# An adaLN transformer block on one core: five steps of a hand-written schedule moved by a slot or a few

## The chip, the core and the metric

The kernel runs on one core of a Trainium2 chip. A core has a matrix engine (PE, with its weight loads shown apart as PEld), a vector engine (DVE), a scalar engine (ACT), a general engine (POOL) and a sync engine (SP), which here issues nearly all DMAs. The metric is the device time of one execution in microseconds (us). Each kernel is run several times; the median of the runs is compared.

## The reference

One block with adaptive LayerNorm: attention over the last 512 cached keys, then a gated feed-forward layer. S is 2048 rows, D is 512, there are 32 query heads and 8 key/value heads of 128, and F is 1792. All is float32.

```python
mod = (silu(c) @ w_mod).reshape(1, 6, 1, 512)
sa, ca, ga, sb, cb, gb = (mod[:, i] for i in range(6))
h = layernorm(x) * (1 + ca) + sa
q = heads(h @ wq)                                   # 32 heads of 128
k, v = k_cache[:, :, -512:, :], v_cache[:, :, -512:, :]   # each serves 4 heads
p = softmax(q @ k.T * 128 ** -0.5)
x = x + ga * (merge(p @ v) @ wo)
h = layernorm(x) * (1 + cb) + sb
x = x + gb * ((gelu(h @ w_gate) * (h @ w_up)) @ w_down)
```

## The kernel before

**Numbers.** Every float32 operand of a large product is split into a high and a low float16 part; `mm3` (line 87, where all the products stand as L91) makes one product of three float16 matmuls. A split is two instructions: the high part is a copy on ACT, the low part a subtraction on DVE or POOL.

**Strassen-like combinations.** The query projection and the feed-forward layer use seven block products for eight. They need the normalised activations in blocks `b11, b21, y, b22` (plain) and `t1, t2, t3, t4` (combined). The activations are written to DRAM as float32 (`hs`), and `combos` (line 570) later loads them back as tiles `cb` (`load`), subtracts them from one another on POOL (`diff`, L582, `cb<-cb`), and splits the results into the blocks (high part on ACT at L380, low part on POOL at L384). `combos(gen, p, ...)` yields four pairs of a load and its steps. `gen` counts uses: 0 and 1 are the first and second 1024 rows for attention, 2 and 3 the first and second 1024 rows for the feed-forward layer; `p` is 0 or 1.

**Attention.** There are 128 units (a head pair's head, a row block of 512) of four slots; slot `t` runs from 0 to 511 (`T` is 512). In a slot PE makes the scores `ps` of 128 rows, DVE takes their maximum (`nm`, L990), ACT the exponential (`ee`, L999) and, two slots later, the high part of the probabilities (`p`, L1011), DVE, three slots later, their low part (L1016), and SP a DMA transpose of both (`pt<-p`, L1020). The DMA transposes are counted T0 to T511 here, one for each slot; T(t-3) is issued in slot t. The product with V (`po`) of a unit needs all four of its transposes and comes two units later. Beside it PE makes the next queries (`qa, qb, qc, pq`) and the output projection (`py`), three groups of matmuls in each slot from a queue.

**Order.** Nothing is left to a scheduler here: `at(("w", t), fn)` puts a step at the end of slot t, on whatever engines its instructions use, and each engine runs its instructions in that order. Loads into pools with few buffers go through `sched(pos, (load, steps), ..., ahead=AHEAD)`: the steps run at the slots given, and the load is issued `ahead` slots (3) before the first one, or when the buffer is released by the numbers of the schedule, if that is later. Pools are served in order of the first step's slot, so a load can wait behind another one. `spare` issues one waiting background DMA (stores of split weights, `kept<-...`, and fetches of them) in a slot that has moved nothing else.

**LayerNorm of the second half.** When the attention output of a row tile `ti` is complete (`attn_final`, slots 256 to 290 for the tiles 0 to 7), `ln_tile(2, ti, ...)` gives seven steps: `stat`, `norm` (POOL), `turn` (four PE transposes into a PSUM bank `pln`, L508), `affine` of columns 0 and 1 and of columns 2 and 3 (two ACT instructions each, `hf<-pln`, L516, the second one also stores to `hs`), and two splits. They are placed at offsets from the slot in which the tile is complete:

```python
for d, fn in zip((1, 5, 8, 9, 10, 12, 13), steps):
    at(("w", now[0] + d), fn)
```

The bank `pln` comes from the pool `acc` of five PSUM banks, which are taken in turn.

**Feed-forward weights.** `prep_set(q, b)` (line 1372) splits one pair of weight blocks (q even: gate, q odd: up) in the slots from `b` on, on ACT, PE, DVE and POOL, into four `stage` tiles, and stores these to DRAM for much later. Its two loads go into the pool `rw`, which has two buffers (`NRW`); the split is `made(k)` on POOL (L159, L160), the last reads of the two buffers are `made(1)` and `made(2)`.

```python
for n in range(NP):
    b = T // 2 + 30 + 27 * n
    prep_set(2 * n, b)
    prep_set(2 * n + 1, b + 13)
    prep_wd(n, b + 21)
```

**Feed-forward.** After slot 512 there are 28 items of seven products each (`fa, fb, fc`), and between them the down projection in two halves of seven products (`ya, yb, yc`). `step(q, fn)` puts a step behind product `q % 7` of item `q // 7`. DVE adds each finished `y` product into `yt` (L1687). The bank `ya` takes part in four products of a half, and PE may go on in it only after DVE has read it. `combos(3, 1, ...)`, the last combinations, are loaded at step 70, for products from step 98 on. DVE forms `gelu(gate) * up` at L1294 (`fg`), POOL the combinations of that at L1320.

Of the kernel before, what the change touches and what calls it, by code (L numbers as in the profile page):

```python
# [26 lines left out]
QT = QB // P  # L27
EPS = 1e-5
SCALE = DH ** -0.5
AHEAD = 3  # L30
# [35 lines left out]
def block_kernel(ctx: ExitStack, tc: tile.TileContext, x, kT, v, wq, wo, wg, wu, wd, cT, wc, wm, out):  # L66
    nc = tc.nc
# [10 lines left out]
    def raw(name):  # L78
        return pool.tile([P, 512], F32, tag="raw", name=name, bufs=NRAW)
# [15 lines left out]
    def dma(out_, in_):  # L95
        moved[0] += 1
        nc.sync.dma_start(out_, in_)
# [276 lines left out]
    def stored(gen, name, p):  # L374
        qb, dt = {"b11": (0, p), "b21": (0, 2 + p), "y": (1, p), "b22": (1, 2 + p)}.get(name, (None, None))
        return spilled(gen, name)[:, p, :] if qb is None else spilled(gen, qb)[:, dt, :]
# [193 lines left out]
    def combos(gen, p, eng, base=True, d=0, e=0):  # L570
        X = {}

        def load(name):
            if gen == 0 and (p == 0 or name in ("b21", "b22")):
                X[name] = kept({"b11": "s1", "y": "u2", "b21": "u3"}[name]) if name != "b22" else \
                    pool.tile([P, 512], F32, tag="w2", name="cb", bufs=2)
            else:
                X[name] = raw("cb")
            dma(X[name], stored(gen, name, p))

        def diff(o, a, b):
            return lambda: nc.gpsimd.tensor_tensor(X[o], X[a], X[b], op=ALU.subtract)  # L582

        def parts(pos, name, tile_):
            high, low = put(gen, name, p, lambda: X[tile_], eng)
            return [(pos, high), (pos + 1 + e, low)]

        def plain(pos, name):
            return parts(pos, name, name) if base else []

        return [
            (lambda: load("b11"), plain(0, "b11") + [(2, diff("b11", "y", "b11"))] + parts(d + 4, "t1", "b11")),
            (lambda: load("y"), [(2, nop), (3, diff("y", "b22", "y"))] + parts(d + 5, "t3", "y")),
            (lambda: load("b22"), (plain(1, "b22") or [(2, nop)]) + [(4, diff("b22", "b22", "b11"))] + parts(d + 6, "t2", "b22")),
            (lambda: load("b21"), plain(3, "b21") + [(5, diff("b21", "b21", "b22"))] + parts(d + 7, "t4", "b21")),
        ]
# [19 lines left out]
    def sched(pos, ld, *more, kind="raw", ahead=AHEAD):  # L616
        loads.append(((pos,) + more, ld, kind, ahead))
# [121 lines left out]
    def at(key, *fns):  # L739
        later.setdefault(key, []).extend(fns)  # L740
# [154 lines left out]
    def kept(k):  # L895
        return pool.tile([P, QB], F32, tag=k, name=k, bufs=1)
# [69 lines left out]
    def attn_final(ti):  # L966
        y1[ti] = dram.tile([P, D], F32, name=f"y{ti}")
        dma(y1[ti], acc[ti])
        if ti < 2 * QT:
            nxt = ti + 2 * QT  # L970
            own, steps = ln_tile(2, ti, lambda: acc[ti])
            own()
            for d, fn in zip((1, 5, 8, 9, 10, 12, 13), steps):
                at(("w", now[0] + d), fn)
            at(now[0] + 12, lambda: load_acc(nxt, rows_of(x, nxt)))
        else:
            ln_last(ti - 2 * QT)
# [204 lines left out]
    def sched_combos(gen, p, base):  # L1182
        for k, (load, steps) in enumerate(combos(gen, p, nc.gpsimd if gen or p == 0 else nc.vector, False, 0 if gen else 1 if p else 2, 0 if gen or p else 5)):
            if gen == 0 and (p == 0 or k > 1):
                at(base + ((0, 0, 0, 2)[k] if p else (-10, -2, -1, -9)[k]), load)
                for off, fn in steps:
                    at(("w", base + off), fn)
            else:
                sched(base + steps[0][0], (load, [fn for _, fn in steps]), *[base + off for off, _ in steps[1:]])

    for p in range(2):
        sched_combos(0, p, CB[p])
# [25 lines left out]
    for g in range(NG):  # L1218
# [6 lines left out]
        if 0 < g < GW:  # L1225
            a, b = plain_steps(g, by)
            sched_pair(g, srcs, t0 - (19 if g > 1 else 13), spread, [(t0 - (13 if g > 1 else 8), a)], [(t0 - (11 if g > 1 else 7), b)])
        elif g >= GW and (not half or pr < GW):
            sched_set(g, srcs, t0, by, spread)
            if not half:  # L1230
                a, b, c, d, e, f = SETPOS2 if g == GW else SETPOS
# [11 lines left out]
        else:  # L1243
            if g > 0:
                if pr % 2 == 0:
                    load, stat, spread_, parts = k_items(pr)
                    sched(t0 - (22 if g > 2 else 20), (load, [stat]))
                    at(("w", t0 - (19 if g > 2 else 17)), spread_)
                load, stat, spread_, parts = k_items(pr)
                sched(t0 - (7 if g > 2 else 8 if g > 1 else 6), (load, [parts if g != 2 else lambda parts=parts: soon(parts(True))]))  # L1250
                at(t0 - (3 if g > 2 else 1 if g > 1 else 2), lambda pr=pr: store(("k", pr), KV[0, pr, 0]))
                if pr % 2 == 0:
                    load, stat, spread_, parts = v_items(qd)
# [118 lines left out]
    def prep_set(q, b):  # L1372
        m, key, by = {}, ("f", q), col("fsc", f_scale(q))
        l, r = slice(0, 256), slice(256, 512)
        outs = [staged() for _ in range(4)]
        srcs = set_srcs(q)

        def tt(o, a, c, op):
            nc.gpsimd.tensor_tensor(o, a, c, op=op)

        def made(k, src):
            halves(outs[k][0]["t"] if k < 3 else outs[k][0]["t"][:, :, 0:256], src)

        def keep_it(k):
            return lambda: store(("w", key, k), outs[k][0]["t"] if k < 3 else outs[k][0]["t"][:, :, 0:256], 0)

        def s0():
            times(RAW[key][0], by)
            made(0, RAW[key][0])

        def s1():
            r1 = RAW[key][1]
            times(r1, by)
            made(3, r1[:, r])
            tt(r1[:, r], r1[:, l], r1[:, r], ALU.add)

        def s2():
            r0, r1 = RAW[key][0], RAW[key][1]
            tt(r1[:, l], r0[:, l], r1[:, l], ALU.subtract)
            tt(r0[:, l], r1[:, r], r0[:, l], ALU.subtract)  # L1400
            tt(r0[:, r], r0[:, r], r0[:, l], ALU.subtract)

        sched(b, (lambda: set_load(key, srcs, 0), [lambda: pair_stat(key, m, 0), nop]), b + 9, kind="rw")
        sched(b + 1, (lambda: set_load(key, srcs, 1), [lambda: pair_stat(key, m, 1), lambda: f_spread(f_scale(q), m["m"]), s2, nop]),
              b + 4, b + 9, b + 10, kind="rw")
        sched(b + 7, (outs[0][1], [s0, keep_it(0)]), b + 10)
        sched(b + 8, (outs[3][1], [s1, keep_it(3)]), b + 11)
        sched(b + 9, (outs[1][1], [lambda: made(1, RAW[key][0]), keep_it(1)]), b + 12)
        sched(b + 10, (outs[2][1], [lambda: made(2, RAW[key][1]), keep_it(2)]), b + 13)
# [65 lines left out]
    for n in range(NP):  # L1475
        b = T // 2 + 30 + 27 * n
        prep_set(2 * n, b)
        prep_set(2 * n + 1, b + 13)
        prep_wd(n, b + 21)
    for n, b in ((NP - 2, T - 57), (NP - 1, T - 22)):  # L1480
        prep_wd(n, b, True)
# [165 lines left out]
    def step(q, fn):  # L1647
        f_at(q // 7, q % 7, fn)

    for i, q in enumerate((16, 19, 22, 26, 30, 33, 36, 40)):  # L1650
        load, norm, split, turn = ln_turned(i)
# [3 lines left out]
        step(q + 4, turn)  # L1655
    for q, (qb, dt) in zip((37, 41, 44, 47, 50, 51, 54, 55), ((0, 0), (0, 2), (0, 1), (0, 3), (1, 0), (1, 2), (1, 1), (1, 3))):
        step(q, lambda qb=qb, dt=dt: turned_out(qb, dt))
    for p, (q, at_) in enumerate(((59, (61, 62, 62, 63, 64, 65, 66, 67, 68)), (70, (75, 76, 76, 79, 80, 81, 82, 89, 90)))):
        for load, steps in combos(3, p, nc.gpsimd):
            step(q, load)  # L1660
            for off, fn in steps:
                step(at_[off], fn)

    def whole(ti):
        if ti in halfway and ti in joined:
# [117 lines left out]
    for q in range(NQ):  # L1783
        n, m = divmod(q, 2)
# [55 lines left out]
```

## Time and profile before

| | |
|---|---|
| median of 3 runs | 1733.44 us (1733.02 to 1733.84) |
| the profiled execution | 1734.19 us, of which 1732.4 us from its first to its last instruction |
| PE busy | 1711.2 us, 99% |
| DVE, ACT, POOL busy | 82%, 72%, 63% |
| granted TensorE clock | 0.999 |
| DMA | 343.51 MB, mean 198 GB/s |

In the timeline a row is: start, duration, engine, line, operation, output<-input and their kind, the number of instructions merged, and in brackets the idle time before it with what ended it. PE's matmuls overlap: their ends are modelled, and a row of three matmuls of 512 columns reads 0.81 us while the next row begins 0.65 us after it. SPq rows are issues of DMAs; a transfer's landing is another number.

### The profile page before, as it was taken

The numbers are of one execution on the slowest core, as the hardware profiler recorded it, in microseconds if no ns is written. First come the engines' busy times: TensorE is split into PE (matmuls) and PEld (weight loads), VectorE is DVE, ScalarE is ACT, GpSimd is POOL, SyncE is SP. The second block draws the span as 40 slices with busy tenths as digits, with TensorE's granted clock in tenths as the row PEclk, the third lists the DMA queues.
The fourth block names the chain that finished last, engine by engine and source line by source line (L and its number), as shares of the span: only waits on it lengthen the run. The fifth ranks groups of instructions, "written<-read, shape, count | busy, mean of one in ns | idle before, by whom it ended". The sixth has DMA issues, their size and how long they took to land.

```text
span 1732.4 us, 26343 instructions
## 1 busy us (share of the span) xinstructions
PE 1711.2 (99%) x8012; PEld 787.1 (45%) x8012; DVE 1425.8 (82%) x2476; ACT 1254.3 (72%) x2819; POOL 1093.3 (63%) x1328
## 2 busy tenths in 40 slices
PE   7999999999999999999999999999999999999998
PEld 5444444444444444444444444444444444444444
DVE  7888898988888899888888888888896788676666
ACT  6988788888888777897787777787785354455442
POOL 4879778777788884655665755747760345735424
PEclk9999999999999999999999999999999999999999
DMA  7999999999999998999999999999997556355353
GB/s 234 218 208 210 214 214 205 225 205 220 211 229 222 206 210 181 219 207 224 198 232 219 206 231 208 203 218 221 229 227 164 163 145 196 118 164 174 96 157 104
DMA packets 693454, 343.51 MB, mean 198 GB/s; under 512 B 579136, under 2 KB 602688, under 8 KB 693312
## 3 DMA queue, kind: packets, MB, share of 16 engines
q1 hardware_dynamic: 693024, 341.30, 85.4%
q8 instruction: 63, 1.03, 0.3%
q14 instruction: 79, 0.65, 0.1%
q10 hardware_dynamic: 288, 0.52, 0.1%
HBM read 137.50 MB, written 63.70 MB: 116 GB/s over the span
## 4 chain that ended last, share of the span: by engine, by line
PE 86%; DVE 5%; ACT 4%; POOL 2%; DMA 2%; issue 1%; SPq 0%; POOLq 0%; DVEq 0%; ACTq 0%
PE py L91 18%; PE po L91 17%; PE ps L91 16%; PE fa L91 8%; PE qa L91 8%; PE fc L91 4%; PE qc L91 4%; PE ya L91 3%; PE fb L91 2%; PE qb L91 2%; PE yc L91 2%; ACT ee L999 1%; DVE p L1016 1%; DVE nm L990 1%; ACT p L1011 1%
## 5 line engine op out<-in xcount | busy, mean ns | idle before, releaser
L999 ACT ACTIVATE ee<-ps,nm 128x512 f32<-128x512 f32 x512 | 349.6, 683 | 184.2 <-DVE nm L990 181.0
L1016 DVE SCALAR_TENSOR_TENSOR p<-ee,rr,p 128x512 f16<-128x512 f32 x512 | 454.1, 887 | 8.1 <-ACT p L1011 7.5
L990 DVE TENSOR_REDUCE nm<-ps 128x1 f32<-128x512 f32 x512 | 350.3, 684 | 105.7 <-PE ps L91 102.9
L91 PE MATMUL ps<-k,qt 128*128 128x512 f16 x1536 | 414.9, 379 | 3.8 <-ACT ee L999 2.5
L1011 ACT ACTIVATE p<-ee,rr 128x512 f16<-128x512 f32 x512 | 363.9, 711 | 21.9 <-DMA pt<-p 11.6
L91 PE MATMUL po<-pt,v 128*128 128x512 f16 x1536 | 372.9, 379 | 2.8 <-DVE kmax L184 1.0
L91 PE MATMUL py<-wo,ot 128*128 128x512 f16 x1536 | 371.3, 379 | 0.0
L91 PEld LDWEIGHTS <-w 128*128 128x128 f16 x2184 | 214.0, 98 | 259.7 <-issue 2.7
L91 PEld LDWEIGHTS <-v 128*128 128x128 f16 x1536 | 149.9, 98 | 185.1 <-issue 5.1
L91 PEld LDWEIGHTS <-ot 128*128 128x128 f16 x1536 | 150.3, 98 | 181.2
L91 PEld LDWEIGHTS <-qt 128*128 128x128 f16 x1536 | 145.8, 98 | 174.8 <-issue 3.3
L1320 POOL TENSOR_TENSOR fg<-fg 128x512 f32<-128x512 f32 x48 | 63.0, 1312 | 147.0 <-DVE fg L1294 144.2
L748 DVE SCALAR_TENSOR_TENSOR ot<-po,ot 128x512 f16<-128x512 f32 x128 | 87.8, 686 | 37.7 <-ACT ot L747 37.3
L1304 ACT ACTIVATE at<-fg 128x512 f16<-128x512 f32 x92 | 56.3, 626 | 80.1 <-DVE fg L1294 61.7
L999 ACT ACTIVATION_READ_ACCUMULATOR ee<-ps,nm 128x1 f32 x512 | 100.1, 195 | 0.0
L960 DVE SCALAR_TENSOR_TENSOR acc<-py,ysc,acc 128x512 f32<-128x512 f32 x128 | 94.7, 740 | 5.3 <-PE py L91 5.3
L91 PE MATMUL qa<-t,w 128*128 128x512 f16 x348 | 84.9, 379 | 0.0
L236 POOL TENSOR_TENSOR lw<-lw,half__86 128x1 f32<-128x1 f32 x39 | 25.0, 641 | 91.0 <-DVE lw L186 91.0
L91 PE MATMUL fa<-t,w 128*128 128x512 f16 x336 | 81.7, 379 | 0.1
L747 ACT ACTIVATE ot<-po 128x512 f16<-128x512 f32 x128 | 73.9, 577 | 5.0 <-PE po L91 5.0
L403 POOL TENSOR_TENSOR rs<-rs,nhalf 128x1 f32<-128x1 f32 x32 | 18.7, 586 | 92.9 <-DVE rs L397 90.0
L91 PEld LDWEIGHTS <-wo 128*128 128x128 f16 x504 | 49.3, 98 | 60.6 <-issue 1.3
(243 smaller groups left out, 2821.9 us busy)
## 6 DMA issues: line engine op xcount, KB each, us to landing
w<-kept SPq DMA_DIRECT2D x123, 256.0 KB, 3.3
wo<-kept SPq DMA_DIRECT2D x72, 256.0 KB, 3.3
kept<-stage SPq DMA_DIRECT2D x67, 256.0 KB, 3.2
raw<-in_wo SPq DMA_DIRECT2D x56, 256.0 KB, 3.2
kept<-w SPq DMA_DIRECT2D x39, 256.0 KB, 3.3
rw<-in_wq SPq DMA_DIRECT2D x38, 256.0 KB, 3.1
hs<-hf SPq DMA_DIRECT2D x32, 256.0 KB, 2.8
pt<-p SPq DMA_TRANSPOSE x512, 3.5
```

Of the source, the lines that this page charges most:

```text
L91: nc.tensor.matmul(ps, a, b, start=first and n == 0, stop=last and n == 2, skip_group_check=chain)
L236: nc.gpsimd.tensor_tensor(out, out, half_, op=ALU.pow)
L403: nc.gpsimd.tensor_tensor(st["rs"], st["rs"], nhalf, op=ALU.pow)
L747: nc.scalar.activation(t[:, 0, :], src, AF.Copy, scale=scale)
L748: return lambda: nc.vector.scalar_tensor_tensor(t[:, 1, :], src, scale, t[:, 0, :], op0=ALU.mult, op1=ALU.subtract)
L960: nc.vector.scalar_tensor_tensor(acc[ti], st["p"], by, acc[ti], op0=ALU.mult, op1=ALU.add)
L990: nc.vector.tensor_reduce(nm, E[t]["ps"], axis=AX.X, op=ALU.max, negate=True)
L999: nc.scalar.activation(e, E[t]["ps"], AF.Exp, bias=E[t]["nm"], scale=1.0, accum_out=sm[:, t % 2:t % 2 + 1])
L1011: nc.scalar.activation(p16[:, 0, :], E[t]["e"], AF.Copy, scale=E[t]["r"])
L1016: nc.vector.scalar_tensor_tensor(p16[:, 1, :], E[t]["e"], E[t]["r"], p16[:, 0, :], op0=ALU.mult, op1=ALU.subtract)
L1304: nc.scalar.activation(t[:, 0, :], g, AF.Copy)
L1320: nc.gpsimd.tensor_tensor(g[o], g[a], g[b], op=ALU.subtract)
```

## The change

Four places of the schedule are edited; no computation is added or taken away, and each engine executes the same instructions as before.

1. In `sched_combos`, the four loads of the combinations of the generations 1 and 2 get their own distances before the first step, 3, 2, 1 and 3 slots, where each had 3.
2. In `attn_final`, for `ti` 2 and 6, the second pair of affine pieces is put in the same slot as the first (offset 9 for 10).
3. The second `prep_set` of n = 0 begins one slot later (`b + 14`); all its steps move by one slot.
4. The steps of `combos(3, 1)` get a table for each of the four tiles. The subtraction into `y` moves from step 79 to 81, that into `b22` from 80 to 82, that into `b21` from 81 to 89; the split of `t3` (`y`) from 81/82 to 83/89, of `t2` (`b22`) from 82/89 to 88/89 and of `t4` (`b21`) from 89/90 to 95/96 (high part / low part).

```diff
             own, steps = ln_tile(2, ti, lambda: acc[ti])
             own()
-            for d, fn in zip((1, 5, 8, 9, 10, 12, 13), steps):
+            for d, fn in zip((1, 5, 8, 9, 9, 12, 13) if ti % QT == QT - 2 else (1, 5, 8, 9, 10, 12, 13), steps):
                 at(("w", now[0] + d), fn)
...
     def sched_combos(gen, p, base):
...
             else:
-                sched(base + steps[0][0], (load, [fn for _, fn in steps]), *[base + off for off, _ in steps[1:]])
+                sched(base + steps[0][0], (load, [fn for _, fn in steps]), *[base + off for off, _ in steps[1:]], ahead=(3, 2, 1, 3)[k] if gen else AHEAD)
...
         prep_set(2 * n, b)
-        prep_set(2 * n + 1, b + 13)
+        prep_set(2 * n + 1, b + (13 if n else 14))
...
-    for p, (q, at_) in enumerate(((59, (61, 62, 62, 63, 64, 65, 66, 67, 68)), (70, (75, 76, 76, 79, 80, 81, 82, 89, 90)))):
-        for load, steps in combos(3, p, nc.gpsimd):
-            step(q, load)
-            for off, fn in steps:
-                step(at_[off], fn)
+    for load, steps in combos(3, 0, nc.gpsimd):
+        step(59, load)
+        for off, fn in steps:
+            step((61, 62, 62, 63, 64, 65, 66, 67, 68)[off], fn)
+    for (load, steps), at_ in zip(combos(3, 1, nc.gpsimd), ((75, 76, 76, 80, 81), (76, 81, 83, 89), (76, 76, 82, 88, 89), (79, 80, 89, 95, 96))):
+        step(70, load)
+        for (_, fn), k in zip(steps, at_):
+            step(k, fn)
```

**Place one: SP around the transposes T197 to T201** (edit 1, generation 1, p = 0). `cb<-hs` are the loads of the combinations, `rw<-in_wq` those of the next query weights, `kept<-wo` a background store. Before:

```order
L1020 DMA_TRANSPOSE pt<-p_7010 128x8x128
L97 DMA cb<-hs_1_5325 128x512
L97 DMA cb<-hs_0_3160 128x512
L97 DMA cb<-hs_1_5325 128x512
L1020 DMA_TRANSPOSE pt<-p_7039 128x8x128
L97 DMA rw<-in_wq 128x512
L97 DMA kept<-wo 128x1024
L1020 DMA_TRANSPOSE pt<-p_7073 128x8x128
L97 DMA rw<-in_wq 128x512
L1020 DMA_TRANSPOSE pt<-p_7108 128x8x128
```

The same place after the change:

```order
L1020 DMA_TRANSPOSE pt<-p_7010 128x8x128
L97 DMA kept<-wo 128x1024
L1020 DMA_TRANSPOSE pt<-p_7039 128x8x128
L97 DMA cb<-hs_1_5325 128x512
L97 DMA cb<-hs_0_3160 128x512
L97 DMA rw<-in_wq 128x512
L1020 DMA_TRANSPOSE pt<-p_7068 128x8x128
L97 DMA cb<-hs_1_5325 128x512
L97 DMA rw<-in_wq 128x512
L1020 DMA_TRANSPOSE pt<-p_7106 128x8x128
```

The four transposes are T197 to T200. The three loads in one gap have become none, two and one in three gaps (the pool's order keeps the first two together), and the store has moved up. Between T197 and T199 stand five other DMAs and T198 before, four and T198 after. In generation 2 the loads around T475 and T485 move by one slot in the same way; with them a weight fetch moves from before T476 to before T479 and a fetch of V from before T479 to before T481. In generation 1, p = 1, nothing moves.

**Place two: ACT and SP around T290 to T296** (edits 2 and 3). First ACT, one piece of the difference, for `ti` 6; the piece for `ti` 2, some 16 slots earlier, reads alike. `hf<-pln` are the affine pieces, `qt` the high part of the next queries:

```order
 L1011 ACTIVATE p_10040<-ee,rr 128x512
-L516 ACTIVATE hf<-pln,cols 128x128 x2
-L999 ACTIVATE ee,sm<-ps,nm 128x512
-L1004 ACTIVATE rr<-sm 128x2
-L1011 ACTIVATE p_10074<-ee,rr 128x512
-L747 ACTIVATE qt<-qd,qsc 128x512
-L516 ACTIVATE hf<-pln,cols 128x128 x2
+L516 ACTIVATE hf<-pln,cols 128x128 x4
+L999 ACTIVATE ee,sm<-ps,nm 128x512
+L1004 ACTIVATE rr<-sm 128x2
+L1011 ACTIVATE p_10075<-ee,rr 128x512
+L747 ACTIVATE qt<-qd,qsc 128x512
```

The third and fourth affine piece now stand ahead of the next exponential. Their store `hs<-hf` moves one transpose earlier on SP. Then SP from T293 to T296 (edit 3); `rw<-in_wu` are the two loads that come a slot later, `kept<-stage` stores of the set prepared before. Before:

```order
L1020 DMA_TRANSPOSE pt<-p_10146 128x8x128
L97 DMA rw<-in_wu 128x512
L97 DMA kept<-stage 128x1024
L97 DMA hs_1_9778<-hf 512x1x128
L1020 DMA_TRANSPOSE pt<-p_10183 128x8x128
L97 DMA rw<-in_wu 128x512
L97 DMA kept<-stage 256x1x256
L1020 DMA_TRANSPOSE pt<-p_10218 128x8x128
L97 DMA acc<-in_x 128x512
L97 DMA kept<-stage 128x1024
```

After:

```order
L1020 DMA_TRANSPOSE pt<-p_10146 128x8x128
L97 DMA kept<-stage 128x1024
L97 DMA hs_1_9778<-hf 512x1x128
L1020 DMA_TRANSPOSE pt<-p_10183 128x8x128
L97 DMA rw<-in_wu 128x512
L97 DMA kept<-stage 256x1x256
L1020 DMA_TRANSPOSE pt<-p_10216 128x8x128
L97 DMA acc<-in_x 128x512
L97 DMA rw<-in_wu 128x512
L97 DMA kept<-stage 128x1024
```

Each `rw` load has moved behind one more transpose; the first store and `hs` no longer stand behind a load. The next set's loads, between T307 and T309, stay where they are, while the steps that release their buffers come one slot later.

**Place three: POOL in items 10 to 13 of the feed-forward** (edit 4). `cb<-cb` are the subtractions, `b` and `t` low parts of blocks, `fg` and `at` the combinations of the gated activations. Before:

```order
L384 TENSOR_TENSOR b_18219<-cb,b_18219 128x512
L582 TENSOR_TENSOR cb<-cb 128x512
L384 TENSOR_TENSOR b_18240<-cb,b_18240 128x512
L582 TENSOR_TENSOR cb<-cb 128x512 x2
L384 TENSOR_TENSOR b_18261<-cb,b_18261 128x512
L384 TENSOR_TENSOR t_18276<-cb,t_18276 128x512
L582 TENSOR_TENSOR cb<-cb 128x512
L384 TENSOR_TENSOR t_18302<-cb,t_18302 128x512
L1320 TENSOR_TENSOR fg<-fg 128x512 x4
```

After:

```order
L384 TENSOR_TENSOR b_18219<-cb,b_18219 128x512
L582 TENSOR_TENSOR cb<-cb 128x512
L384 TENSOR_TENSOR b_18240<-cb,b_18240 128x512
L384 TENSOR_TENSOR b_18261<-cb,b_18261 128x512
L384 TENSOR_TENSOR t_18276<-cb,t_18276 128x512
L582 TENSOR_TENSOR cb<-cb 128x512 x2
L1320 TENSOR_TENSOR fg<-fg 128x512 x4
```

The two subtractions that stood together ahead of the low parts `b_18261` and `t_18276` stand together behind them; the third one and the remaining low parts come behind the combinations of the gated activations.

## The prediction

> **What bounds the kernel now.** First the page's busy shares, then the window from 100 us (behind the start) to 1720 us; the columns are the span, then busy time of PE, PEld, DVE, ACT and POOL, the granted clock, the DMA share and GB/s.
>
> ```profile
> PE 1711.2 (99%) x8012; PEld 787.1 (45%) x8012; DVE 1425.8 (82%) x2476; ACT 1254.3 (72%) x2819; POOL 1093.3 (63%) x1328
> 100.00:1720.00 1620.00, 1616.30 (x7566) 736.86 (x7564) 1338.99 (x2294) 1176.28 (x2640) 1029.93 (x1235) 1.00 0.86 197
> ```
>
> PE sets the time, and its matmuls are the same before and after. All that a reordering can win behind the start is PE's idle time, 1620.00 - 1616.30 = 3.70 us by the page. So the question is which waits make that up. PE's own list of waits (total, times, longest) names the places; the first edit that moves an instruction stands near 535 us, so the start stays as it is.
>
> ```profile
> PE ps L91 <- ACT ee L999: 2.5, 4, 1.9
> PE po L91 <- DVE kmax L184: 1.0, 1, 1.0
> PE ya L91 <- DVE yt L1687: 0.8, 1, 0.8
> PE pln L508 <- POOL w L159: 0.6, 1, 0.6
> ```
>
> The first of these belongs to the start. I then read the timeline at each pause of PE. I measure a pause from row to row: three matmuls give a row of 0.81 us, but the next row normally starts 0.65 us after it, so what exceeds 0.65 is lost, 0.16 more than the bracket says.
>
> **Edit 1, the loads one per slot.** The timeline of PE, SP and DVE near 540 us, and the landing times of the eight transposes from 530 to 550 us and of T199 alone (T199 is the row at 540.28):
>
> ```profile
> 535.92 1.48 SPq L97 DMA_DIRECT2D cb<-hs  x3
> 540.28 3.52 SPq L1020 DMA_TRANSPOSE pt<-p  x1
> 541.15 0.75 DVE L748 SCALAR_TENSOR_TENSOR qt<-qb,qsc,qt 128x512 f16<-128x512 f32 x1 [0.16 <-ACT qt L747]
> 545.47 0.81 PE L91 MATMUL ps<-k,qt 128*128 128x512 f16 x3
> 547.28 2.10 PE L91 MATMUL po<-pt,v 128*128 128x512 f16 x9 [1.01 <-DVE kmax L184]
> DMA to landing us min/median/max: 3.1/4.3/7.2
> DMA to landing us min/median/max: 6.8/6.8/6.8
> ```
>
> PE could have started `po` at 545.47 + 0.65 = 546.12 and started at 547.28: 1.16 us lost. The bracket blames `kmax` on DVE, which frees the bank of the small product just before. I don't believe it: the banks of that pool go round in fives, and five back (`po`, the small one, `py`, `po`, `py`, `qb`) is `qb`, last read by DVE at 541.15. T199 lands at 540.28 + 6.8 = 547.1 us, which fits. It was held behind three loads issued at once, and took 6.8 us where 3.1 is the least. The change takes one load from in front of T199 (front of the list: five other DMAs before, four after). The excess in the worst transpose, 7.2 - 3.1 = 4.1 us, shared by the three loads, gives 1.4 us each; at least 256 KB at the window's 197 GB/s, 1.3 us (estimate). T199 would land at about 545.7, ahead of 546.12. I take the whole 1.16 us; bounds 0 (the queue is full anyway) and 1.16. Behind it T200 to T203 have as many DMAs ahead as before. POOL's subtractions wait for loads about a slot later and have the slots up to the use of the blocks; the fetches of weights and of V moved in generation 2 (by two or three slots) still come at least three slots before their products. PE has no pause worth a row there. Cost nothing.
>
> **Edit 2, four affine pieces together.** PE and ACT at the two tiles:
>
> ```profile
> 730.21 0.81 PE L91 MATMUL po<-pt,v 128*128 128x512 f16 x3
> 731.65 0.63 PE L508 MATMUL pln<-ident,acc 128*128 128x128 f32 x4 [0.63 <-POOL w L159]
> 770.79 0.79 ACT L516 ACTIVATE hf<-pln,cols 128x128 f32<-128x128 f32 x2
> 773.38 0.81 PE L91 MATMUL po<-pt,v 128*128 128x512 f16 x3
> 773.58 0.80 ACT L516 ACTIVATE hf<-pln,cols 128x128 f32<-128x128 f32 x2
> 774.51 0.63 PE L508 MATMUL pln<-ident,acc 128*128 128x128 f32 x4 [0.32 <-ACT hf L516]
> ```
>
> The next tile's transposes wait for the bank, and the bank for the last piece: 773.58 + 0.80 = 774.38, PE goes on at 774.51. Lost: 774.51 - 774.03 = 0.48 us; at the first tile, by the same pattern, 731.65 - 730.86 = 0.79. After the change the four pieces end near 770.79 + 0.79 + 0.80 = 772.4, 1.6 us before they are needed. The price is 0.80 us on ACT ahead of the exponential, the reciprocal's input, `p` and `qt` of that slot; ACT has 0.80 us less in the next slot, and the scores that need this exponential's bank come two slots later. I take 0.79 + 0.48 = 1.27 us; bounds 0 (ACT's delay comes back) and 1.27.
>
> **Edit 3, two weight loads a slot later.** SP, POOL and PE:
>
> ```profile
> 785.30 2.01 SPq L1020 DMA_TRANSPOSE pt<-p  x1
> 787.22 0.62 POOL L159 TENSOR_SCALAR stage<-rw 128x512 f16<-128x512 f32 x1 [3.84 <-DMA kept<-stage]
> 787.92 1.53 POOL L160 TENSOR_TENSOR stage<-rw,stage 128x512 f16<-128x512 f32 x1
> 789.49 0.36 SPq L97 DMA_DIRECT2D rw<-in_wu  x1
> 790.53 1.32 SPq L1020 DMA_TRANSPOSE pt<-p  x1
> 793.11 0.81 PE L91 MATMUL ps<-k,qt 128*128 128x512 f16 x3
> 794.47 2.10 PE L91 MATMUL po<-pt,v 128*128 128x512 f16 x9 [0.55 <-DMA pt<-p]
> ```
>
> SP ends T294 at 787.31 and stands until 789.49: the load needs the buffer that POOL reads until 787.92 + 1.53 = 789.45. T295, at 790.53, stands behind it, and PE waits: 794.47 - 793.76 = 0.71 us lost. After the change the load ahead of T295 is the set's first, whose buffer POOL has left before 787.22; T295 can go up to 789.49 - 787.31 = 2.2 us earlier, three times what is needed. POOL's wait of 3.84 us for a store shrinks too, since that store no longer stands behind a load. I take 0.71; bounds 0 and 0.71. All else of this set (two squares on ACT, a small product on PE, two small steps on DVE, the split on POOL, four stores) comes a slot later, for weights used in the feed-forward. What becomes tight is the next set, which loads at its old slot:
>
> ```profile
> 817.61 1.16 POOL L160 TENSOR_TENSOR stage<-rw,stage 128x512 f16<-128x512 f32 x1
> 818.79 0.34 SPq L97 DMA_DIRECT2D rw<-in_wg  x1
> 819.82 1.31 SPq L1020 DMA_TRANSPOSE pt<-p  x1
> 827.28 1.23 SPq L1020 DMA_TRANSPOSE pt<-p  x1
> 834.68 1.67 PE L91 MATMUL po<-pt,v 128*128 128x512 f16 x7
> ```
>
> POOL's read, ending at 818.77, moves back by a slot (T308 to T311: 7.46 / 3 = 2.5 us) to 821.3, and SP stands there with T308 behind it. T311, at 827.28, is then at most 2.5 us late and lands, by the median 4.3 above, at 834.1, still ahead of `po` at 834.68. Cost nothing, but the cover is only 0.6 us.
>
> **Edit 4, the last combinations.** POOL, DVE and PE in item 11:
>
> ```profile
> 1485.00 2.61 POOL L582 TENSOR_TENSOR cb<-cb 128x512 f32<-128x512 f32 x2
> 1486.36 1.81 DVE L1294 SCALAR_TENSOR_TENSOR fg<-fg,gsc,fu 128x512 f32<-128x512 f32 x1
> 1487.95 0.81 PE L91 MATMUL yb<-at,wo 128*128 128x512 f16 x3
> 1489.53 0.81 PE L91 MATMUL ya<-at,wo 128*128 128x512 f16 x3 [0.77 <-DVE yt L1687]
> 1493.76 0.81 DVE L1294 SCALAR_TENSOR_TENSOR fg<-fg,gsc,u 128x512 f32<-128x512 f32 x1
> 1495.16 0.74 DVE L1687 SCALAR_TENSOR_TENSOR yt<-ya,dyc,yt 128x512 f32<-128x512 f32 x1
> 1496.65 0.81 PE L91 MATMUL ya<-at,wo 128*128 128x512 f16 x3
> ```
>
> The same instruction took 1.81 us beside POOL's two subtractions and 0.81 at 1493.76: 1.00 us of DVE, and PE lost 1489.53 - 1488.60 = 0.93 behind it. After the change POOL has nothing there until the next low part. The Trainium skill, page "SBUF — State Buffer", section "Who interferes with whom", says that a DVE instruction with two SBUF inputs and a GpSimd instruction that reads SBUF exclude each other for a whole instruction, and the first one wins. The rows at 1485.00 and 1486.36 agree. I take 0.93; bounds 0 (rival below) and 0.93. The later splits end at step 96 for products from step 98 on, on a POOL that has gaps.
>
> **The sum.** 1.16 + 1.27 + 0.71 + 0.93 = 4.07 us, five pauses; their brackets and 0.16 each are the page's idle time almost whole. I take back 0.2 us for new small waits (the gap between the bracket 0.55 and the loss 0.71 shows how roughly such rows read). The profiled execution would go from 1734.19 to 1730.3; the median lies 0.75 below it, so 1733.44 - 3.87 = 1729.6 us. A measurement of this kernel can tell about 0.2%, 3.5 us, from no change: the forecast lies just beyond.
>
> **The rivals.**
> (a) The pause moves with the pair of subtractions. They still stand together, now among DVE's steps from 1493.76 on. If one of them starts just ahead of that `fg`, DVE loses 1.00 again; `yt` ends at 1495.90 and PE needs it at 1496.65, 0.75 later, so PE would lose 0.25; behind both, up to 0.93. Time at worst: 1729.6 + 0.9 = 1730.5. The skill's rule named above is what would do it. For it: the pair. Against: in the new order a low part runs ahead of the pair and DVE may get in first.
> (b) The DMA queue is full anyway, so edits 1 and 3 only shift late transposes: 1729.6 + 1.16 + 0.71 = 1731.5. For it: the DMA share of 0.86. Against: the least landing in the window around T199, 3.1, shows that the queue does empty between the bursts.
> (c) ACT's 0.80 in front of the exponential comes back as a wait for scores: 1729.6 + 1.27 = 1730.9.
> (d) Several of these at once, no net change: about 1733.4.
> (e) Slower: the tight place goes from T295 to T308. If two of POOL's four split pieces there also wait 3.84 us for a buffer, as the one at 787.22, T311 is 2.5 + 7.7 = 10.2 us late where 834.68 - 827.28 - 3.1 = 4.3 are to spare: PE stands for 5.9 us. A pause of 1.9 us at the start (list of waits above) goes with a lower granted clock there:
>
> ```profile
> 80.00:120.00 40.00, 37.37 (x166) 16.35 (x166) 34.54 (x64) 35.54 (x88) 28.18 (x38) 0.96 1.02 216
> ```
>
> That is 0.04 x 40 = 1.6 us more: 1729.6 + 5.9 + 1.6 = 1737.1. It decides from a delay of 4.3 + 3.9 = 8.2 us on. Against: no wait for a buffer stands in front of POOL's read at 817.61.
>
> **How the numbers follow.** Forecast 0.56, between 1729.0 and 1730.3; (a) 0.15, (b) 0.11, (c) 0.07, (d) 0.06, (e) 0.05. Faster by over 0.2% means under 1729.97: four fifths of the forecast's case, 0.45. Slower by over 0.2%: (e), 0.05. The rest, 0.50, is within 0.2%. The range holds the forecast, (a), (b) and (c), which is 0.89 by my count; the unknown ends of the costs are inside it: 1728.8 to 1732.2.
>
> **What would show it.** Right: PE idle between 100 and 1720 us under 1 us; `po` of the place at 547 without a pause and T199 landing in under 6 us; no wait of `pln` for `hf` at the two tiles; SP not standing before T295; the `fg` of item 11 at 0.75 to 0.81 us. Wrong: a PE pause of 0.5 us or more at a new place, above all at `po` after T308 to T311, at `ya` in item 11's second half, or at the scores behind the four affine pieces.

## The result, and the profile after

The changed kernel takes 1730.30 us (median of 22 runs, 1729.17 to 1732.23) against 1732.94 us for the kernel before on the same chip (22 runs, 1731.42 to 1734.63): 2.6 us less, a ratio of 0.9985 with an interval of 0.9979 to 0.9991. That is inside the 0.2% that counts as no change here. 3.9 us were forecast. The profiled execution took 1731.43 us, 1729.6 of them span.

The kernel after: first the busy shares of the page, then the window from 100 to 1720 us (columns as in the prediction), then PE's list of waits in that window.

```profile
PE 1709.0 (99%) x8012; PEld 786.6 (45%) x8012; DVE 1426.7 (82%) x2476; ACT 1254.7 (73%) x2819; POOL 1090.0 (63%) x1328
```

```profile
100.00:1720.00 1620.00, 1618.06 (x7576) 738.00 (x7574) 1342.55 (x2297) 1176.25 (x2640) 1028.46 (x1236) 1.00 0.86 197
```

```profile
PE po L91 <- DMA pt<-p: 0.9, 1, 0.9
PE fa L91 <- ACT fg L893: 0.4, 1, 0.4
PE ps L91 <- ACT ee L999: 0.3, 2, 0.2
```

PE's idle time in the window fell from 3.70 to 1.94 us; under 1 us was forecast. Three waits of the list before are gone (`pln` for `w` and for `hf`, `ya` for `yt`). A wait of `po` for a transpose is still there, and one of the scores `ps` for the exponential `ee` has grown.

Site by site. **Edit 1**, the timeline of SP and PE near 540 us, and behind it the time to landing of T199 alone (the row at 540.38):

```profile
537.44 2.36 SPq L97 DMA_DIRECT2D cb<-hs  x2
540.38 1.23 SPq L1020 DMA_TRANSPOSE pt<-p  x1
545.06 0.81 PE L91 MATMUL ps<-k,qt 128*128 128x512 f16 x3
546.81 2.12 PE L91 MATMUL po<-pt,v 128*128 128x512 f16 x9 [0.94 <-DMA pt<-p]
```

```profile
DMA to landing us min/median/max: 6.4/6.4/6.4
```

One load less stands in front of T199, and yet it takes 6.4 us instead of 6.8; under 6 was forecast. PE loses 546.81 - 545.71 = 1.10 us where it lost 1.16. The bracket now names the transpose itself, so the forecast's reading of who is waited for (not `kmax`) was right.

**Edit 2**, the timeline of PE, ACT and DVE at the first of the two tiles:

```profile
727.36 1.49 ACT L516 ACTIVATE hf<-pln,cols 128x128 f32<-128x128 f32 x4
730.40 0.60 PE L508 MATMUL pln<-ident,acc 128*128 128x128 f32 x4
733.49 0.67 DVE L138 SCALAR_TENSOR_TENSOR wmc<-wmc,sbc 128x512 f32<-128x512 f32 x1
734.09 0.68 DVE L990 TENSOR_REDUCE nm<-ps 128x1 f32<-128x512 f32 x1
734.81 0.69 ACT L999 ACTIVATE ee<-ps,nm 128x512 f32<-128x512 f32 x1 [1.77 <-DVE nm L990]
738.12 0.69 ACT L999 ACTIVATE ee<-ps,nm 128x512 f32<-128x512 f32 x1
738.94 0.81 PE L91 MATMUL ps<-k,qt 128*128 128x512 f16 x3 [0.17 <-ACT ee L999]
```

The four pieces stand together and `pln` starts without a wait. But 8 us later the scores wait for an exponential, and ACT had itself stood 1.77 us waiting for a maximum from DVE, which came to it only behind another step, a multiplication of `wmc`.

**Edit 3**, the timeline of SP and PE near 790 us, and **edit 4**, that of POOL and DVE in item 11, both of the kernel after:

```profile
787.16 1.32 SPq L1020 DMA_TRANSPOSE pt<-p  x1
792.09 0.81 PE L91 MATMUL ps<-k,qt 128*128 128x512 f16 x3
792.73 2.11 PE L91 MATMUL po<-pt,v 128*128 128x512 f16 x9
...
1484.30 0.75 DVE L1294 SCALAR_TENSOR_TENSOR fg<-fg,gsc,fu 128x512 f32<-128x512 f32 x1
1490.78 0.81 DVE L1294 SCALAR_TENSOR_TENSOR fg<-fg,gsc,u 128x512 f32<-128x512 f32 x1
1491.00 3.07 POOL L582 TENSOR_TENSOR cb<-cb 128x512 f32<-128x512 f32 x2
```

T295 goes out at 787.16 instead of 790.53 (PE is 1.0 us ahead there by its scores, so 2.35 us of this are the edit's), and `po` follows the scores after 0.64 us, without a pause. `fg` takes 0.75 us instead of 1.81, and the pair of subtractions in its new place is the one that is held up (3.07 us for two that took 2.61), not DVE.

For comparing many kernels a pause is measured here as follows: in the flow two matmuls of 512 columns start 0.216 us apart, and what consecutive starts exceed this by, summed over a place, is the loss there in us. The last matmul of the two profiled executions starts at 1727.67 and 1724.99 us, 2.68 apart. The places, before and after:

| place | 546 | 731 | 738 to 768 | 774 | 792 | 800 to 1330 | 1487 | behind 1500 |
|---|---|---|---|---|---|---|---|---|
| before | 1.17 | 0.80 | 0 | 0.48 | 0.71 | 0.62 | 0.94 | 0.74 |
| after | 1.12 | 0 | 0.78 | 0 | 0 | 0.30 | 0 | 1.04 |

So of five pauses two stay as losses: the one of edit 1, and the larger one of edit 2 under another name. Edits 3, 4 and the second tile bring 0.71 + 0.94 + 0.48 = 2.13 us; the rest of the 2.68 lies at the start (where the instructions are the same) and at small pauses that come and go.

### The profile page after: what moved, and what is told of

Same layout as the page of the kernel before. It is cut to its first block, busy times and chain, and to the rows that moved or that the text cites. A ratio compares the mean times of both kernels' runs of the same rounds, so it can differ in the third digit from the quotient of the medians.

```text
span 1729.6 us, 26339 instructions
## 1 busy us (share of the span) xinstructions
PE 1709.0 (99%) x8012; PEld 786.6 (45%) x8012; DVE 1426.7 (82%) x2476; ACT 1254.7 (73%) x2819; POOL 1090.0 (63%) x1328
## 4 chain that ended last, share of the span: by engine, by line
PE 88%; DVE 4%; ACT 3%; DMA 2%; POOL 1%; issue 1%; SPq 0%; POOLq 0%; ACTq 0%; DVEq 0%
PE py L91 19%; PE po L91 17%; PE ps L91 17%; PE fa L91 8%; PE qa L91 8%; PE fc L91 4%; PE qc L91 4%; PE ya L91 3%; PE fb L91 2%; PE qb L91 2%; PE yc L91 2%; DMA pt<-p 1%; DVE p L1016 1%; ACT ee L999 1%; DVE nm L990 1%
```

## The experiments

Twelve more kernels, one of them the kernel after once more, ran with a profile and with timing. The times tell apart little (an interval is 2 to 3 us wide), so the pauses of the profiled executions carry most of the argument; here they are for all kernels, by the same measure (the 5.44 of `rel` stand at 780 us):

| kernel | 546 | 731 | 738 to 768 | 774 | 792 | 1487 | ratio to before |
|---|---|---|---|---|---|---|---|
| after | 1.12 | 0 | 0.78 | 0 | 0 | 0 | 0.9985 [0.9979, 0.9991] |
| after, once more (`again`) | 0 | 0 | 0.65 | 0 | 0 | 0 | 0.9986 [0.9978, 0.9995] |
| edit 1 undone (`no1`) | 0.93 | 0 | 0.75 | 0 | 0 | 0 | 0.9993 [0.9984, 1.0003] |
| edit 2 at the second tile only (`no2a`) | 0 | 0.78 | 0 | 0 | 0 | 0 | 0.9984 [0.9975, 0.9994] |
| edit 3 undone (`no3`) | 0.29 | 0 | 0.66 | 0 | 1.71 | 0 | 0.9997 [0.9988, 1.0006] |
| edit 4 undone (`no4`) | 0 | 0 | 0.79 | 0 | 0 | 0.92 | 0.9989 [0.9979, 0.9999] |
| before with edit 1 alone (`e1`) | 0 | 0.68 | 0 | 0.46 | 0.79 | 0 | 0.9996 [0.9987, 1.0005] |
| before with edits 3 and 4 (`e34`) | 1.23 | 0.79 | 0 | 0.46 | 0 | 0 | 0.9995 [0.9986, 1.0004] |
| three loads behind T199 (`late`) | 0 | 0 | 0.79 | 0 | 0 | 0 | 0.9995 [0.9986, 1.0004] |
| second rows stored by blocks (`lay`) | 0 | 0 | 0.65 | 0 | 0 | 0 | 0.9985 [0.9976, 0.9995] |
| sixth column moved (`rel`) | 0.82 | 0 | 0 | 0 | 5.44 | 0 | 1.0017 [1.0007, 1.0026] |
| the same, own buffers (`relw`) | 0 | 0 | 0 | 0 | 0 | 0 | 0.9986 [0.9977, 0.9995] |
| `relw` and `lay` (`best`) | 0 | 0 | 0 | 0 | 0 | 0 | 0.9981 [0.9972, 0.9990] |

**Edit 1 undone (`no1`).**

```diff
-  ..., ahead=(3, 2, 1, 3)[k] if gen else AHEAD)
+  ...)
```

> The changed kernel with edit 1 undone (all combination loads three slots ahead again). Forecast's theory (each load in front of T199 costs it 1.3 us): the pause of PE at po near 546 us is as before the change, 1.16 us, and the time is at least 0.8 us above the changed kernel's. New theory (T199 is late because the loads from hs take about 2 us each in the queue and the queue has a hole of 1.5 to 2 us there, and one load fewer in front doesn't change that): the pause is within 0.3 us of the changed kernel's 1.11 us, and the other pauses are as in the changed kernel.

The pause at 546 us is 0.93 us, hardly different from that of the kernel after. On this one pair edit 1 would be worth nothing.

**Edit 2 at the second tile only (`no2a`).**

```diff
-  ... if ti % QT == QT - 2 else ...
+  ... if ti == QT + QT - 2 else ...
```

> The changed kernel with edit 2 for tile 6 alone, so tile 2's second pair of affine pieces is a slot later again. Theory of the give-back (DVE and its chain of maximum, exponential and scores pace the stretch from 725 to 770 us, and PE runs into them when its pause at 731 goes): the pause of pln at 731 is back with 0.8 us, the waits of the scores at 738, 760, 766 and 768 us (0.77 us together in the changed kernel) go, and the time is that of the changed kernel within 0.3 us. Rival (those waits come and go by chance): they stay, and the span is 0.8 us longer.

The pause of `pln` at the first tile is back, 0.78 us, the four small waits at 738 to 768 us are gone, and the second tile stays free of its pause. The same amount is lost either way: at the first tile edit 2 gains nothing.

**The sixth modulation column out of the stretch (`rel`).** The stretch of 728 to 770 us also holds DVE's multiplications for the sixth column (L138, `wmc`) and the maximum of its row. They were put 20 to 24 slots later, and the four loads of `wmc` with them.

```diff
-  (5, (274, 278, 282, 286))
+  (5, (298, 301, 304, 307))
...
-    at(T // 2 + 34, lambda: mod_row(5))
+    at(T // 2 + 54, lambda: mod_row(5))
```

> The changed kernel with five DVE steps taken out of the stretch from 725 to 770 us: the four products for the last modulation vector go from slots 274 to 286 to slots 298 to 307, its row and maximum from slot 290 to 310. Give-back theory (DVE paces the stretch): the waits of the scores from 738 to 768 us fall from 0.77 us to 0.3 or less, and the span is some 0.5 us shorter. Rival (ACT's four affine pieces ahead of the exponential are what the scores wait for): the waits stay, since ACT's work there is the same.

The four waits at 738 to 768 us are gone, as hoped, but PE then stands at 780 us. The timeline of POOL, ACT and PE there, and behind it two windows (columns as above; the granted clock is the third from the end):

```profile
774.68 3.47 POOL L1379 TENSOR_TENSOR rw<-rw 128x256 f32<-128x256 f32 x4
778.25 0.93 POOL L159 TENSOR_SCALAR stage<-rw 128x512 f16<-128x512 f32 x1
782.62 0.81 ACT L516 ACTIVATE hf<-pln,cols 128x128 f32<-128x128 f32 x2 [5.32 <-DMA kept<-stage]
784.14 1.15 PE L91 MATMUL ps<-k,qt 128*128 128x512 f16 x3 [3.59 <-ACT ee L999]
```

```profile
780.00:784.00 4.00, 0.55 (x3) 0.15 (x2) 0.00 (x0) 1.38 (x5) 0.42 (x1) 1.00 0.53 131
784.00:788.00 4.00, 3.86 (x11) 1.38 (x11) 2.43 (x4) 3.97 (x11) 0.00 (x0) 0.57 0.33 86
```

The affine pieces `hf` take a buffer from the same ring of five as the staged weights `stage` and the pieces `wmc`. With the moved pieces the turn falls on a buffer that is still being split and stored, and ACT stands 5.32 us at the head of the chain to the scores. That is 3.76 us of PE (3.973 between two starts, less 0.216); and then the granted clock is 0.57 for 4 us, in which nine matmuls start 0.30 to 0.43 us apart instead of 0.216. The whole place costs 5.44 us, 1.7 of it by the clock.

**The same with two buffers of its own (`relw`).**

```diff
-        t = raw("wmc")
+        t = pool.tile([P, 512], F32, tag="mc", name="wmc", bufs=2) if j == 5 else raw("wmc")
...
```

> The run rel with one thing mended: the four pieces of the sixth modulation column (loads, VectorE multiplications and the row after them some 24 slots later, out of the stretch of 733 to 765 us) come from two buffers of their own, not from the ring of five that the staged weights and the second rows share. Theory (rel lost 3.8 us because the affine pieces wait at 780 us for a buffer of that ring, and 1.7 us more because the clock halves for 3.4 us after the wait; and the stretch of 728 to 770 us is paced by VectorE): the wait at 780 us and the half clock are gone, the waits of 0.77 us at 738, 760, 766 and 768 us stay away as in rel, no pause comes at 794 us; 0.5 to 0.8 us faster than the changed kernel, 1729.6 us. Rival (the loads at slots 298 to 307 themselves cost it, through SyncE's queue): a wait of 1 us or more is back between 775 and 800 us, 1731 us or more.

Both are gone: the wait at 780 us, and the waits at 738 to 768 us. The window from 728 to 770 us for before, then after, then `relw`:

```profile
728.00:770.00 42.00, 41.37 (x203) 19.95 (x202) 37.16 (x71) 37.23 (x93) 22.68 (x25) 1.00 0.95 220
```

```profile
728.00:770.00 42.00, 41.67 (x203) 20.04 (x202) 36.28 (x69) 36.50 (x91) 21.40 (x24) 1.00 0.94 217
```

```profile
728.00:770.00 42.00, 42.00 (x205) 20.19 (x204) 35.91 (x68) 37.21 (x93) 22.34 (x24) 1.00 0.94 211
```

PE is without a gap only in the third. With the extra work in the stretch some 0.8 us are lost whether PE waits early (before) or in small portions (after); without it nothing is lost. That it is DVE's part of this work that counts, and not the loads, is read from DVE's waits in the window: for its maximum it waited for scores from PE 0.9 us before, never in the kernel after, and 2.7 us in `relw`. So only in the kernel after was DVE behind PE throughout. The time itself, 1730.19 us, is that of the kernel after: the profiled execution of `relw` had a new pause of 0.49 us at 860 us and others, 1.32 us between 800 and 1330 us in all.

**Edits 3 and 4 undone (`no3`, `no4`).** The diffs are those of the change, backwards; first edit 3, then edit 4.

> The changed kernel with edit 3 undone: the second set of item 0 is prepared from slot b + 13 again, one slot earlier. Theory (edit 3 removed the pause of 0.71 us at 794 us by taking a load out of the way of T295): the pause of 0.6 to 0.8 us in front of po is back at 791 to 793 us, with the transpose in front of it landing later than the pause's start; the other places as in the changed kernel; 0.7 us slower than the changed kernel, 1731.0 us. Rival (the pause was chance, like the ones at 1136 and 1196 us that went away untouched): no pause there, 1730.3 us.

> The changed kernel with edit 4 undone: the steps of the last combinations stand in the old slots. Theory (edit 4 is worth the whole pause): the pause of 0.9 us in front of ya is back at 1484 to 1486 us, released by DVE's yt, and nothing else differs; 0.9 us slower than the changed kernel, 1731.2 us. Rival (POOL's and DVE's chains near the end would have had slack in most executions): under 0.3 us of pause there, 1730.3 to 1730.5 us.

Without edit 3 the pause at 792 us is back with 1.71 us, more than the 0.71 of before, with POOL standing 3.9 us for a store and T295 going out at 789.22, behind the load again. Without edit 4 `ya` waits 0.92 us again. In all executions: 0.71, 1.71 and 0.79 us without edit 3, none in ten with it (`rel` apart, which stops at 780 us). The medians go the same way: `no3` takes 1731.75 us and `no4` 1731.43, 1.5 and 1.1 us more than the kernel after, though each interval against before is wide.

**Three loads behind T199 (`late`).**

```diff
-  ahead=(3, 2, 1, 3)[k] ...
+  ahead=((1, 1, 1, 3) if gen == 1 and p == 0 else (3, 2, 1, 3))[k] ...
```

> The changed kernel, with the loads cb of the first of the two sets of second rows (generation 1, p = 0) one slot in front of their use at the earliest, so that three of them that stand in front of transpose T199 go behind it. Theory A (the pause at 546 us follows what stands in front of T199 in the queue): T199 lands in under 5 us and the pause of 1.1 us is gone; 1.0 us faster than the changed kernel in the profiled run. Theory B (the pause comes from the hole of some 1.5 us in the throughput of all queues that follows an instruction fetch, where it falls between the issue of T198 and the landing of T199): T199 still lands 6 us after its issue where the hole comes within 3 us of it, and the pause is 0.8 to 1.1 us; no difference to the changed kernel. Against both: the combinations then wait for their own late loads, a pause of 0.5 us or more at 548 to 560 us.

T199 lands 3.6 us after its issue and the pause at 546 us is gone, though a long fetch of an instruction block (1.3 us, more on these below) begins 1.5 us behind T198. So what stands in front of T199 does count, in this one execution. But the combinations now wait for their loads: 0.37 us at 554 us and 0.71 us at 563 us, 1.07 together. It is no gain.

**The second rows stored block by block (`lay`).** A load `cb` reads 2 KB out of every 8 KB of a partition's row in `hs`; here each block lies in one piece.

```diff
-            hs[gen, key] = dram.tile([P, n, QB], F32, ...)
+            hs[gen, key] = dram.tile([n, P, QB], F32, ...)
...
```

> The changed kernel with hs stored block by block in DRAM, so that a combination load reads 256 KB in one piece and not 2 KB out of every 8 KB. If the slow loads are what holds T199: a load from hs takes about 1.0 us in the queue where it took 1.8, T199 lands 1.5 to 2 us earlier, the pause at 546 us goes and the span is 1.1 us shorter. If the hole in the queue alone does it, or the loads are slow for another reason: landing times of cb stay at 4.3 us, the pause stays within 0.3 us of 1.11.

From 535 to 547 us the four loads land in 3.9 us in the median, against 5.7 us in the kernel after (the lists of DMA issues of that window, after and then `lay`: number, size, median to landing), and there is no pause at 546 us. The pause proves nothing for the layout, since the kernel after had none either in executions with as short a fetch (0.95 us here). The landing does: over 500 to 1400 us the median of all sixteen loads is 3.4 us here and 3.3 in `best`, and 4.0 to 4.2 in the twelve profiles with the old layout. The two lists from 535 to 547 us:

```profile
cb<-hs SPq DMA_DIRECT2D x4, 256.0 KB, 5.7
```

```profile
cb<-hs SPq DMA_DIRECT2D x4, 256.0 KB, 3.9
```

The time is that of the kernel after; this profiled execution lost 2 us in its first 100 us, where the granted clock was 0.62 from 26 to 30 us.

**The kernel after once more, and edit 1 alone and left out (`again`, `e1`, `e34`).** By now the pause at 546 us had come and gone in kernels with the same instructions there.

> The changed kernel once more. Theory (the pause at 546 us depends on where the instruction fetch falls against the issue of T198: a fetch of 1.3 us or more some 1.4 us behind it gave 1.1 and 0.8 us, a fetch of 0.9 to 1.0 us at 1.8 us or more behind it gave 0 to 0.3 us): the pause is 0.8 to 1.1 us if the fetch takes 1.3 us or more, else 0 to 0.3 us; none at 731, 774, 794 and 1488 us; four small waits of 0.75 to 0.8 us together at 738 to 768 us; 1730.3 us.

> The kernel before with edit 1 alone. Theory: pauses of 0.79, 0.48 and 0.94 us at 731, 774 and 1488 us as before, one of 0.7 to 1.7 us at 794 us, none at 738 to 768 us; at 546 us 0 to 0.3 us with a short fetch, 0.8 to 1.1 us with a long one; 0.4 to 0.8 us faster than before on the mean of such executions, within the spread of the times. Rival (edit 1 does nothing at all): 0.9 to 1.2 us at 546 us whatever the fetch.

> The kernel before with edits 3 and 4 alone. Theory: no pause at 794 and 1488 us, 0.79 and 0.48 us at 731 and 774 us, none at 738 to 768 us, and at 546 us 0.9 to 1.2 us as in both executions without edit 1; 1.6 us faster than before, 1731.3 us. Rival (without edit 1 the pause at 546 us is as often absent as with it): under 0.3 us there.

Without edit 1 the pause is 1.17, 0.93 and 1.23 us (before, `no1`, `e34`). With it, in the same layout and order, it is 1.12, 0, 0, 0.29, 0, 0.82, 0 and 0 (after, `again`, `no2a`, `no3`, `no4`, `rel`, `relw`, `e1`), 0.28 in the mean. So edit 1 is worth about 0.8 us on the average of these eleven executions, and the profile after was one of its two bad ones. The medians allow it: `no1` takes 1731.47 us, 1.2 more than the kernel after, and `e1` 1731.64, 1.1 less than the kernel before on its chip (1732.78). What differs is a dip in the transfers. GB/s in steps of 0.1 us and the instruction queue (packets, MB, share of 16 engines' time), for the kernel after from 537 us and for `again` from 538 us:

```profile
GB/s 287 287 307 244 190 358 210 200 205 197 74 3 0 0 0 0 0 0 0 5 8 10 8 10 10 10 10 220 289 292 289 354 184 246 287 123 266 246 164 82
q8 instruction: 1, 0.02, 2.2%
```

```profile
GB/s 220 195 202 207 369 192 212 154 79 23 0 0 0 3 8 10 8 8 10 10 10 95 393 410 492 389 20 287 328 266 226 369 307 184 102 102 123 123 123 184
q8 instruction: 1, 0.02, 1.5%
```

An instruction block of 16 KB is fetched, and about half a microsecond after the fetch begins all transfers nearly stop, for 1.7 us in the one and 1.3 us in the other. The fetch itself takes 2.2% of 64 us, 1.4 us, in the one and 1.0 us in the other. With edit 1, all fetches of 1.3 us or more at this place went with a pause of 0.8 us or more (after, `rel`) unless T199 had fewer loads in front (`late`); those of 0.9 to 1.0 us with at most 0.29. Without edit 1, fetches of 0.9 to 1.0 us, some 3 us later against the transposes, were enough for 0.93 to 1.23 us. Why a fetch is long, and why it came later there, was not found.

In `e1`, with the old order, the pause of edit 4's place is missing too. The timelines of POOL and DVE of before and then of `e1`:

```profile
1486.35 1.27 POOL L582 TENSOR_TENSOR cb<-cb 128x512 f32<-128x512 f32 x1
1486.36 1.81 DVE L1294 SCALAR_TENSOR_TENSOR fg<-fg,gsc,fu 128x512 f32<-128x512 f32 x1
```

```profile
1482.58 3.15 POOL L582 TENSOR_TENSOR cb<-cb 128x512 f32<-128x512 f32 x2
1483.84 0.75 DVE L1294 SCALAR_TENSOR_TENSOR fg<-fg,gsc,fu 128x512 f32<-128x512 f32 x1
```

In before, POOL's second subtraction starts 0.01 us ahead of DVE's `fg`, and DVE is held for 1.06 of its 1.27 us. In `e1` DVE comes first, `fg` takes 0.75 us, and the two subtractions take 3.15 instead of 2.61. The Trainium skill, page "SBUF — State Buffer", section "Who interferes with whom", says that the issue order decides who blocks, and both traces agree. Old order: held in two of three executions (before, `no4` with 1.79 us, not `e1`).

**Both mended (`best`).**

> relw and lay together: the changed kernel with the sixth modulation column out of the stretch paced by VectorE, in two buffers of its own, and the second rows kept block by block, so that a load cb reads 256 KB in one piece. Theory: no pause at 546, 731, 738 to 768, 774, 794 and 1488 us; against the changed kernel 0.77 us from the stretch and 0.4 to 1.1 us from the pause at 546 us, less some 0.4 us for new chance pauses: 1729.3 us. Rival (what goes at these places comes back at places that the fetches hit later, as the 0.49 us at 860 us of relw): no difference to the changed kernel, 1730.3 us.

No pause is left at any of the six places, and PE is idle for 0.50 us between 100 and 1720 us:

```profile
100.00:1720.00 1620.00, 1619.50 (x7586) 738.82 (x7585) 1343.93 (x2299) 1175.63 (x2640) 1029.70 (x1235) 1.00 0.86 197
```

It takes 1729.62 us (11 runs) where `again`, beside it on the same chip, takes 1730.93 (11 runs). It is faster than the kernel before, 0.9981 [0.9972, 0.9990]; its interval overlaps that of the kernel after. Run against run on that chip, though, `best` is the shorter in 109 of 121 pairs, so a gain over the kernel after is likely, of a size that is not settled.

## Why the prediction was right, and where it was wrong

The time came within 0.7 us of the forecast, partly by luck: the gain was 2.6 us where 3.9 were forecast, but the three runs that it was subtracted from lay 0.5 us above the median of all 22. The mechanisms of edits 3 and 4 and of the second tile were right. Two terms of the sum were mis-sized, and one was right by less than it seemed.

- **Edit 1, 1.16 us forecast; 0.05 in the profiled pair, 0.8 by the means of three executions without it and eight with it.** The step that failed is the price of a load in front of T199, (7.2 - 3.1) / 3 = 1.4 us each. It took the three loads as the whole cause of a slow landing. With one load less T199 landed 0.4 us sooner, not 1.4. The rest stands in the trace as a dip of the transfers behind a fetch, 1.7 us in the kernel after, which the trace before also held (the transfers fell behind a fetch at 541 us) and which was not looked for. As far as the eleven executions show, one load less shifts the odds of T199 being caught in it; that the dip is the cause was argued from where it stands, not tried.
- **Edit 2, first tile: 0.79 us forecast, 0 in all executions.** The step "ACT has 0.80 us less in the next slot, and the scores that need this exponential's bank come two slots later" looked two slots ahead on ACT. DVE was the one behind; PE reached it 0.79 us sooner and waited for 0.65 to 0.79 us in four portions up to 768 us. This is rival (c) in its effect (a wait for scores), for this tile alone; `no2a` and `relw` show it, DVE's `wmc` step ahead of the maximum being what was in the way. Second tile: 0.48 us forecast, 0.46 to 0.48 found.
- **Edit 3, 0.71 us forecast; 0.71 to 1.71 us.** Right, and worth more than its one row showed. Rival (e) did not come: POOL's read that was to move to 821.3 ended at 818.83, which against PE, 1.7 us ahead there, is 1.8 us later instead of 2.5; T311 goes out at 827.01, 1.45 us later against PE, and `po` follows without a pause. Its price of 1.6 us for the clock is about the 1.7 us of `rel`, where the drop came behind a wait of 3.76 us; the drop of the very window that it rested on cost nothing (last section).
- **Edit 4, 0.93 us forecast; 0.94 in the pair, but 0.6 in the mean of three executions of the old order**, since in one of them DVE came first. Rival (a) did not come: the pair stands beside DVE's steps, and it is POOL that is held.
- **Rival (b)** (the queue is full anyway) fell: in `late` T199 lands in 3.6 us and the pause at 546 us is gone by what stands in the queue, and edit 3 moved T295.

With the means, 0.83 + 0 + 0.47 + 1.07 + 0.62 = 3.0 us; the runs gave 2.6 us, with 1.6 to 3.6 inside the interval. The sum of pauses of one execution (4.07) was too high mainly because it took every pause of one trace as present in every execution, and counted one that was only passed on.

## What to carry to other kernels

A pause in one profile is one draw: before pricing its removal, ask whether a tenth of a microsecond of another order, or a fetch that falls elsewhere, would have removed it too. When a wait is taken from an engine that is almost full, follow its next rounds on the engine that is slowest there, not two steps on the one that was waited for: the time saved is given back where that engine is reached. And before moving a step, look which ring its buffers come from: four small pieces moved by 21 to 24 slots cost 5.4 us through a ring that they shared.

## What the runs showed of the hardware

Instructions are fetched by DMA while the kernel runs: 63 blocks of 16 KB in the kernel after, 22 to 31 us apart, and on a second queue 79 of 8 KB. Between 100 and 1320 us, 40 of the 46 fetches of 16 KB are followed within 3 us by a stretch of 1 us in which all transfers of the core together stay under 60 GB/s, where the mean is 213; of the 314 stretches of 3 us with no such fetch in them or in the 3 us before, 45 hold such a one. Behind the blocks of 8 KB it is 26 of 60. That the fetch causes the dip was not tried. The Trainium skill, page "Runtime: NRT & Kernel Launch", section "Instruction fetch mechanics", gives blocks of 16 KiB and calls crossing into the next one mostly hidden. For the engines this trace agrees: PE is idle for 1.94 us in all from 100 to 1720 us. It is the other transfers that nearly stop, for 1.7 and 1.3 us in the two dips shown, and with a transpose in the way such a dip went with up to 1.2 us of PE.

The clock drop is not a fixed price. `rel` paid 1.7 us for one behind a full PE, while in the kernel before a drop at 83 to 87 us (granted clock 0.57 in that window) cost nothing: at the same matmul behind it, the kernel after, without a drop, was no further on, since there PE waits for others anyway: its lead was 0.42 us at 78 us, 1.94 us at 87 us and 0.41 us at 99 us.

```profile
83.00:87.00 4.00, 4.00 (x12) 1.50 (x11) 4.00 (x7) 3.04 (x9) 3.82 (x4) 0.57 1.16 321
```

```profile
83.00:87.00 4.00, 3.67 (x17) 1.54 (x16) 4.00 (x8) 3.05 (x8) 3.74 (x5) 1.00 0.90 256
```

The first row is before, the second after: 12 matmuls against 17 in the same 4 us.
